# A gated pair's GELU, two block stores and the wo loads of a fused mixer kernel: four edits in the queues of ScalarE, SyncE and GpSimd

## The chip, the cores and the metric

One core of a Trainium2 chip runs the kernel. The metric is the device time of one execution in microseconds. The engines are named as in the profile: PE is TensorE (matmul; PEld is its weight load), DVE is VectorE, ACT is ScalarE, POOL is GpSimd, SP is SyncE, which here only issues transfers. Each engine executes its own queue strictly in order, as the timelines show: an instruction that waits holds up all behind it on that engine.

## What is computed

Two mixers work on the same normalised input, and their sum is added to the input. Cut to what matters:

```python
xn = layernorm(x)                                   # x: 2048 x 512
# A: linear attention, 32 heads of 16
q, k, v = split(xn @ wqkv)
phi(q) = [softmax(q w_phi), softmax(-q w_phi)]      # per head; the same for k
o = phi(q) (phi(k)^T v) / (phi(q) sum(phi(k)))
# B: gated MLP with a spatial matrix
z  = gelu(xn @ w_in)                                # 2048 x 1376
z1, z2 = z[:, :688], layernorm(z[:, 688:])
g  = w_sp @ z2 + b_sp                               # 2048 x 2048 times 2048 x 688
out = x + o @ wo + (z1 * g) @ w_out
```

All is float32. A product is made of three matmuls: each operand is split into a rounded part (`h`, made by ScalarE with a copy to float32r, `round_h`) and the rest (`l`, made by VectorE with a subtraction, `rest_l`), and `mm3` (L51) adds h·h, h·l and l·h.

## The kernel before, in words

The 2048 tokens are 16 tiles of 128. Up to about 300 us the kernel makes the projections of both mixers: `z2` stays on chip (split, as `B`), `z1` before its GELU goes to memory (`z1_d`), and the query features with their sums go to memory as `e_d`.

**The spatial stage** (L790 to L820, about 300 to 506 us) computes `w_sp @ z2` for eight pairs of token tiles, `i` = 0 to 7. One pair is done in four steps of `n` (`NQ`), each over four of the 16 source tiles; a step has seven products `g` in the manner of Strassen (`FORM`, L682), two blocks each, so 42 matmuls. The seven sums of a pair stand in seven of eight PSUM banks. For step `n` + 2 the weights are prepared by `prep_a` (L516): sums of blocks on VectorE (`S`, L530 to L534), then four pieces that ScalarE rounds and VectorE subtracts (`b_parts`, L503); the last piece is `A22`. The weights `wf` are loaded three steps ahead by SyncE (`load_a`, L507). The prepared weights have two sets of buffers, used in turns.

After a pair's fourth step `drain` (L706) takes the seven sums out of PSUM: ScalarE copies the first (L711), VectorE does the rest (L712 to L718). That frees the banks for the next pair, whose first product uses the eighth bank. Then `gate` (L721) applies GELU to the pair's `z1` on ScalarE (L724), multiplies on VectorE (L727), splits the last 48 of the 688 columns into a rounded part and a rest (L728 to L732), and transposes in blocks of 32 (L733). Its `store` writes the result to memory (`u_d`) in four transfers of 32 partitions, each made of runs of 32 numbers (L738). `load_z1` (L689) brings the next pair's `z1` by two transfers from GpSimd into the one buffer `z1t`; since the transposed block of the pair before stands in the same buffer, the load waits for that store.

**The transition.** During the last steps the weights of `w_out` are staged (`stage_w`, L779), and the blocks of the first tiles are loaded (`first_gate`, L766; `first_q`, L774). The store of pair 6 is put off to step `NC` − 2 and issued by SyncE after the loads of `et` (L819). After the spatial stage SyncE loads `u` of tiles 2 and 3 (`fetch_u`, L921), then `wo` in four transfers of 256 KB with a rearranged source (L929); ScalarE and VectorE split each quarter (L930, L931).

**The output stage** (L945 on) goes over the tiles in pairs: `project_u` multiplies the gated block by `w_out` (17 matmuls into `pout`), `attend_T` transposes the query features on TensorE (`ptq`, L863), `attend` multiplies them by the key-value sums (`po`, 32 small matmuls) and splits the result as `oT`, and `project_o` (L902) adds `oT @ wo` (12 matmuls a tile) and writes the tile out. VectorE finishes the features three tiles ahead (`features`, L837), GpSimd copies them to rounded tiles (`er`, L845), and `u` is loaded four tiles ahead. The last pair, 7, is gated late, after tile 9 (`GATE_LAST`, L966); its block, stored by SyncE, is loaded again as `u` of tiles 14 and 15.

**What sets the order.** The launch builds the program with `schedule_with_timeline_sim=True` (L1000): the place of an instruction in its engine's queue comes from a planner that simulates the program, taking the order of the calls as priority. `tc.issue_after(x)` ties instructions behind `x` in the queue of `x`'s engine. So a moved call can land elsewhere in a queue than its line suggests.

Of the kernel before, what the change touches and what calls it, by code (L numbers as in the profile page):

```python
# [10 lines left out]
F32 = mybir.dt.float32  # L11
F32R = mybir.dt.float32r
# [6 lines left out]
P = 128  # L19
S, D, H, DH, FH = 2048, 512, 32, 16, 688  # L20
# [4 lines left out]
NF = 2 * D  # L25
KF = FH // P
REM = FH - KF * P
FU = FH + REM
BL = 32
# [3 lines left out]
NP = NT // 2  # L33
HP, QP = P // 2, P // 4
# [3 lines left out]
def mixer(ctx: ExitStack, tc: tile.TileContext, x, x_t, wv, wqkT, phi_bd, wo, w_in, wst, b_r, w_out, out):  # L38
    nc = tc.nc
    pe, act, dve, pool, sp = nc.tensor, nc.scalar, nc.vector, nc.gpsimd, nc.sync  # L40


    def round_h(eng, h, src):
        if eng is act:
            return act.activation(h, src, AF.Copy).ins  # L45
        return eng.tensor_copy(h, src).ins

    def rest_l(l, src, h, eng=None):
        return (eng or dve).tensor_tensor(l, src, h.bitcast(F32), op=ALU.subtract).ins  # L49
# [19 lines left out]
    e_d = dram.tile([NT, P, NF + 2 * H], F32, name="e_d")  # L69
# [96 lines left out]
    with ExitStack() as p0:  # L166
# [71 lines left out]
        xt, v, rounded, ready = {}, {}, [], []  # L238
# [131 lines left out]
        t = xz.tile([P, 2, FH], F32R, tag="xz", name="xT")  # L370
        xT.append(t)
        x0, pts = xt.pop(0), []
        for k in range(2):
            pts.append(ps.tile([P, 2, P], F32, tag="mm", name="pt"))
            for c in range(2):
                i = pe.transpose(pts[k][:, c], x0[:, (2 * k + c) * P:(2 * k + c + 1) * P], ident).ins
            keep(pe=i)
        warm_up(2)
        for cs, pt in zip(halves, pts):
            src = pt.rearrange("p a b -> p (a b)")  # L380
            i = round_h(act, t[:, 0, cs], src)
# [7 lines left out]
        p = ps.tile([P, D], F32, tag="mm", name="proj")  # L389
# [7 lines left out]
        p = ps.tile([P, D], F32, tag="mm", name="proj")  # L397
# [18 lines left out]
        p = ps.tile([P, D], F32, tag="mm", name="proj")  # L416
# [60 lines left out]
    QW = NF + 7 * H  # L477

    def load_q(s, et):
        load_q.last = sp.dma_start(et[:, :NF + 2 * H], e_d[s]).ins  # L480
        return et

    def q_fin(et, tmp, zb):
# [13 lines left out]
    NQ = NT // QC  # L497
# [3 lines left out]
    SEQ = [(i, q) for i in range(NP) for q in (range(NQ) if i < NP - 1 else (1, 2, 3, 0))]  # L501

    def b_parts(h, l, src):  # L503
        round_h(act, h, src)
        rest_l(l, src, h)

    def load_a(n):  # L507
        i, q = SEQ[n]
        f = []
        for k in range(2):  # L510
            t = ws.tile([P, QC, P], F32, tag=f"f{k}", bufs=2, name="wf")
            sp.dma_start(t, wst[2 * i + k, :, q * QC:(q + 1) * QC, :])
            f.append(t.rearrange("p (k two) t -> p two k t", two=2))
        return f

    def prep_a(n, f):  # L516

        a, b = f
        pl = hl[n % 2]
        ops = {}  # L520

        def parts(names, src):
            t = pl.tile([P, 2, len(names), 2, P], F32R, tag="".join(names), name="A")
            b_parts(t[:, 0], t[:, 1], src)
            for k, m in enumerate(names):
                ops[m] = t[:, 0, k], t[:, 1, k]

        sums = ws.tile([P, 4, 2, P], F32, tag="S", name="S")
        parts(("A11", "A12"), a)
        dve.tensor_tensor(sums[:, 0], b[:, 0], b[:, 1], op=ALU.add)  # L530
        dve.tensor_tensor(sums[:, 1], sums[:, 0], a[:, 0], op=ALU.subtract)  # L531
        parts(("S1", "S2"), sums[:, 0:2])
        dve.tensor_tensor(sums[:, 2], a[:, 0], b[:, 0], op=ALU.subtract)
        dve.tensor_tensor(sums[:, 3], a[:, 1], sums[:, 1], op=ALU.subtract)  # L534
        parts(("S3", "S4"), sums[:, 2:4])
        parts(("A22",), b[:, 1:2])
        return ops
# [3 lines left out]
    with ExitStack() as p1:  # L541
# [45 lines left out]
        for s in range(NE):  # L587
            et = load_q(s, tb.tile([P, QW], F32, tag="et", bufs=2, name="et"))
# [58 lines left out]
    for s in range(NT):  # L647
        p = zproj((kv_ps_p, zc, zbp, za)[s % 4], s, w2, (0, 1) if s % 2 == 0 else (1, 0))
        n = s // 2
        if s % 2 == 0:  # L650
            z2[n] = zw.tile([P, 4, FC], F32, tag="z2", bufs=2, name="z2")
        z = z2[n][:, 2 * (s % 2):2 * (s % 2) + 2]
# [8 lines left out]
        r = zw.tile([P, 1], F32, tag="rstd", bufs=2, name="rstd")  # L661
# [23 lines left out]
    gt = mid.enter_context(right("gt", 1))  # L685
# [20 lines left out]
    def drain(i, g, cb):  # L706
        g = {k: t[:, :FC] for k, t in g.items()}
        b1, b2 = (bias[:, 2 * i + k:2 * i + k + 1] for k in range(2))
        c11, c12, c21, c22 = (cb[:, k, j] for k in range(2) for j in range(2))
        add = lambda o, p, b, q: dve.scalar_tensor_tensor(o, p, b, q, op0=ALU.add, op1=ALU.add)  # L710
        first = act.activation(c12, g["P1"], AF.Copy)  # L711
        add(c11, g["P2"], b1, c12)  # L712
        dve.tensor_tensor(c21, g["P6"], c12, op=ALU.add)
        dve.tensor_tensor(c12, g["P5"], c21, op=ALU.add)
        dve.tensor_tensor(c21, g["P7"], c21, op=ALU.add)  # L715
        add(c22, g["P5"], b2, c21)
        add(c12, g["P3"], b1, c12)
        drained = add(c21, g["P4"], b2, c21)  # L718
        return cb, first.ins, drained.ins

    def gate(i, cb, z, u, ut):  # L721
        cb, first, _ = cb
        with tc.issue_after(first):
            act.activation(z[:, :, :FH], z[:, :, :FH], AF.Gelu_apprx_tanh)  # L724
        zs = z[:, :, :FH].rearrange("p k (j f) -> p k j f", j=2)
        us = u[:, :, :FH].rearrange("p k (j f) -> p k j f", j=2)
        dve.tensor_tensor(us, zs, cb, op=ALU.mult)  # L727
        rm = slice(KF * P, FH)  # L728
        rh = gt.tile([P, 2, REM], F32R, tag="rh", name="rh")
        dve.tensor_copy(rh, u[:, :, rm])  # L730
        rest_l(u[:, :, FH:FH + REM], u[:, :, rm], rh)
        dve.tensor_copy(u[:, :, rm], rh.bitcast(F32))  # L732
        dve.transpose(ut.rearrange("p k f -> p (k f)"), u.rearrange("p k f -> p (k f)"))  # L733

        def store():
            src = ut.rearrange("p k f -> p (k f)")
            dst = u_d[2 * i:2 * i + 2].rearrange("k (j a) t -> a (k j) t", a=BL)
            for b in range(0, P, BL):  # L738
                sp.dma_start(dst[:, :, b:b + BL], src[b:b + BL].rearrange("p (m b) -> p m b", b=BL))

        return store

# [3 lines left out]
    def load_w(src, parts, h, l, t):  # L746
        rows = 0
        for r0, r1 in parts:
            sp.dma_start(t[rows:rows + r1 - r0], src[r0:r1, :])
            rows += r1 - r0  # L750
        return round_h(act, h, t[:rows]), rest_l(l, t[:rows], h)
# [37 lines left out]
    g, es, ets = {}, {}, {}  # L789
    for n in range(NC):  # L790
        i = SEQ[n][0]
        if n % NQ == 1 and i < NP - 1:
            z = load_z1(i)
        products(n, g)
        if n % NQ == NQ - 1 and i < NP - 1:
            c = gt.tile([P, 2, FU], F32, tag="c", name="c")
            cq = c[:, :, :FH].rearrange("p k (j f) -> p k j f", j=2)
            store = gate(i, drain(i, g, cq), z, c, z)
            if i < NP - 2:
                store()  # L800
            g = {}
        if n + 3 < NC:
            raw[n + 3] = load_a(n + 3)
        if n + 2 < NC:
            A[n + 2] = prep_a(n + 2, raw.pop(n + 2))
        if n == NC - 4:
            stage_w()
        if n == NC - 3:
            zs = slot("zb", F32R)
            zb, ident_r = zs[:, :NF].bitcast(F32), zs[:, NF:NF + P]  # L810
            round_h(act, ident_r, ident)
            sp.dma_start(zb, zb_d)
            uT = [first_gate(0)]
            es[0], es[1] = first_q(0), first_q(1)
        if n == NC - 2:
            t = slot("u1", F32R)
            us = {1: load_u(1, k_tiles(t[:, :KF * P]).bitcast(F32), t[:2 * REM, KF * P:(KF + 1) * P])}
            ets[2], ets[3] = (load_q(s, slot("et")) for s in (2, 3))
            with tc.issue_after(load_q.last):  # L819
                store()  # L820
    cb = drain(NP - 1, g, slot("c").rearrange("p (k j f) -> p k j f", k=2, j=2))
    with tc.issue_after(cb[1]), tc.issue_after(cb[2]):
        es[2], last = q_fin(ets.pop(2), slot("qtmp")[:, :NF], zb)
# [4 lines left out]
    gt = p2.enter_context(right("gl", 1))  # L828
    cw = ctx.enter_context(left("cw", 1))
# [3 lines left out]
    def fetch_u(i):  # L833
        return load_u(i, cw.tile([P, KF, P], F32, tag="u", bufs=4, name="u"),
                      cw.tile([2 * REM, P], F32R, tag="rt", bufs=6, name="rt"))
# [82 lines left out]

    GATE_LAST = 8

    for s in (2, 3):  # L921
        us[s] = fetch_u(s)
    wo_h, wo_l = (cw.tile([P, ND, D], F32R, name=f"wo{k}") for k in "hl")
    p = {0: project_u(0, uT.pop(0))}
    fT = attend_T(0)
    with tc.issue_after(lasts[5]), tc.issue_after(lasts[1]), tc.issue_after(fin[-1]):
        for c in range(ND):
            t = cw.tile([P, D], F32, tag="wof", bufs=4, name="wof")
            sp.dma_start(t, wo.rearrange("(k m a r) d -> k a m r d", k=2, a=2, r=QP)[c // 2, c % 2])  # L929
            round_h(act, wo_h[:, c], t)  # L930
            rest_l(wo_l[:, c], t, wo_h[:, c])  # L931
    p[1] = project_u(1, uT.pop(0))
    oT, ins = attend(fT)
    fin.append(ins)
# [10 lines left out]
    for i in range(0, NT, 2):  # L945
# [15 lines left out]
        if i == 2:  # L961
            with tc.issue_after(lasts[6]):
                z = load_z1(NP - 1)
# [40 lines left out]
```

## Time and profile before

| | us |
|---|---|
| median of 3 runs | 653.47 (652.96 to 654.95) |
| the profiled execution, its own time | 652.16 |
| its span, first to last instruction | 650.4 |
| GpSimd busy | 86.2 |
| ScalarE busy | 269.0 |

The time outside the span is 1.8 us. Busy time is a sum over the engine's instructions; matmuls overlap and their ends are modelled, so a busy TensorE is not TensorE at its peak. In a row of a timeline the first number is the start in us from the span's start, the second the time taken, then come engine, line of the kernel, operation, output and input, the count, and in brackets the idle time before it with what ended that. In a row of waits stand the time waited in total, how often, and the longest. In a row of stretches stand the stretch, its length, the busy time of PE, PEld, DVE, ACT and POOL with counts, the granted share of TensorE's clock, the busy share of the 16 DMA engines, and GB/s. In a row of transfers the last number is the median time from issue to landing.

### The profile page before, as it was taken

What the parts mean: (1) busy time and instruction counts of PE and PEld (TensorE: products, weight loads), DVE (VectorE), ACT (ScalarE), POOL (GpSimd) and SP (SyncE); (2) the same over time, 40 slices, a digit from 0 to 9 for tenths busy, and PEclk for the clock granted to TensorE, in tenths of its full rate; (3) what the DMA queues carried; (4) which work ended last, traced back from release to release, by engine and by line L of the source; (5) the groups of instructions that cost most, each with busy time, mean ns of one, the idle gap of its engine ahead of it and who ended that gap; (6) DMA issues with size and microseconds to landing.
All of it is one profiled execution on the core that took longest, in us unless ns stands there. A gap on an engine that the chain in (4) does not pass through costs nothing.

```text
span 650.4 us, 11408 instructions
## 1 busy us (share of the span) xinstructions
PE 627.9 (97%) x4406; PEld 569.9 (88%) x4406; DVE 518.4 (80%) x916; ACT 269.0 (41%) x431; POOL 86.2 (13%) x168
## 2 busy tenths in 40 slices
PE   8999999999999999999999998998999769999998
PEld 6888888888889999999999898998999657777776
DVE  5999979987977699899969678595968569899822
ACT  5643434433324558785343233343335222323220
POOL 4143212111011034440000000000000000100000
PEclk9999999999999999999999998999899969999999
DMA  8345554444356920014455363735559768986921
GB/s 326 141 98 139 134 159 140 112 133 124 88 156 185 324 91 1 2 34 136 102 140 108 129 147 99 163 83 142 104 169 292 174 203 278 316 275 226 248 97 36
DMA packets 94725, 98.39 MB, mean 151 GB/s; under 512 B 52208, under 2 KB 65264, under 8 KB 94672
## 3 DMA queue, kind: packets, MB, share of 16 engines
q1 hardware_dynamic: 84752, 62.81, 34.8%
q0 software_dynamic: 7616, 29.23, 15.2%
q10 hardware_dynamic: 2304, 5.64, 2.3%
q8 instruction: 34, 0.56, 0.3%
q14 instruction: 19, 0.16, 0.1%
HBM read 56.37 MB, written 26.61 MB: 128 GB/s over the span
## 4 chain that ended last, share of the span: by engine, by line
PE 86%; DMA 7%; DVE 3%; issue 2%; SPq 1%; ACT 1%; POOL 0%; ACTq 0%; POOLq 0%; DVEq 0%
PE g L53 9%; PE g L55 9%; PE g L54 9%; PE proj L55 7%; PE proj L53 7%; PE proj L54 7%; PE zps L55 6%; PE zps L53 6%; PE zps L54 6%; PE pout L53 4%; PE pout L54 4%; PE pout L55 4%; DMA wof<-in_wo 2%; DMA z1t<-z_d 2%; DMA et<-e_d 1%
## 5 line engine op out<-in xcount | busy, mean ns | idle before, releaser
L53 PE MATMUL g<-B,A 128*128 128x344 f32 x448 | 145.0, 324 | 6.6 <-DVE c L715 6.6
L54 PE MATMUL g<-B,A 128*128 128x344 f32 x448 | 144.6, 323 | 0.0
L55 PE MATMUL g<-B,A 128*128 128x344 f32 x448 | 144.2, 323 | 0.0
L53 PEld LDWEIGHTS g<-B,A 128*128 128x128 f32 x448 | 85.3, 190 | 8.0 <-DVE c L715 8.0
L54 PEld LDWEIGHTS g<-B,A 128*128 128x128 f32 x448 | 85.3, 190 | 0.0
L55 PEld LDWEIGHTS g<-B,A 128*128 128x128 f32 x448 | 85.3, 190 | 0.0
L45 ACT ACTIVATE A<-S 128x512 fp32r<-128x512 f32 x64 | 39.4, 627 | 70.7 <-DVE S L531 53.0
L49 DVE TENSOR_TENSOR A<-wf,A 128x512 fp32r<-128x512 f32 x64 | 35.4, 554 | 22.8 <-ACT A L45 22.5
L113 ACT ACTIVATE e<-e,r_x 128x1024 f32<-128x1024 f32 x28 | 32.2, 1150 | 49.9 <-DVE e L112 49.9
L53 PE MATMUL proj<-wqk_h,xT 128*128 128x512 f32 x128 | 50.9, 398 | 0.0
L55 PE MATMUL proj<-wqk_h,xT 128*128 128x512 f32 x128 | 50.6, 395 | 0.0
L54 PE MATMUL proj<-wqk_l,xT 128*128 128x512 f32 x128 | 50.3, 393 | 0.0
L49 DVE TENSOR_TENSOR A<-S,A 128x512 fp32r<-128x512 f32 x64 | 43.9, 687 | 7.2 <-ACT A L45 7.0
L53 PE MATMUL zps<-w_0h,xT 128*128 128x344 f32 x128 | 41.4, 323 | 0.0
L55 PE MATMUL zps<-w_0h,xT 128*128 128x344 f32 x128 | 41.1, 321 | 0.0
L53 PE MATMUL zps<-w_1h,xT 128*128 128x344 f32 x128 | 41.0, 320 | 0.0
L55 PE MATMUL zps<-w_1h,xT 128*128 128x344 f32 x128 | 40.9, 320 | 0.0
L54 PE MATMUL zps<-w_0l,xT 128*128 128x344 f32 x128 | 40.9, 319 | 0.0
L54 PE MATMUL zps<-w_1l,xT 128*128 128x344 f32 x128 | 40.9, 319 | 0.0
L45 ACT ACTIVATE A<-wf 128x512 fp32r<-128x512 f32 x64 | 31.8, 514 | 15.3 <-issue 7.2
L116 DVE TENSOR_REDUCE sm<-e 128x64 f32<-128x1024 f32 x28 | 33.9, 1211 | 4.9 <-ACT e L113 4.8
L53 PE MATMUL pout<-woh,oT 128*128 128x512 f32 x60 | 24.6, 410 | 9.9 <-ACT oT L45 9.9
(208 smaller groups left out, 1400.2 us busy)
## 6 DMA issues: line engine op xcount, KB each, us to landing
wf<-in_wst SPq DMA_DIRECT2D x64, 256.0 KB, 3.8
e_d<-e POOLq DMA_DIRECT2D x16, 544.0 KB, 5.2
et<-e_d SPq DMA_DIRECT2D x16, 544.0 KB, 5.5
zacc<-e POOLq DMA_DIRECT2D x12, 512.0 KB, 4.7
er<-et POOLq DMA_DIRECT2D x12, 512.0 KB, 4.9
z_d<-z1f ACTq DMA_DIRECT2D x16, 344.0 KB, 2.2
z1t<-z_d POOLq DMA_DIRECT2D x16, 344.0 KB, 6.0
u_d<-z1t SPq DMA_DIRECT2D x28, 184.0 KB, 4.5
```

The source lines that it names most:

```text
L45: return act.activation(h, src, AF.Copy).ins
L49: return (eng or dve).tensor_tensor(l, src, h.bitcast(F32), op=ALU.subtract).ins
L53: pe.matmul(dst, ah, bh, start=start, stop=False)
L54: pe.matmul(dst, ah, bl, start=False, stop=False)
L55: return pe.matmul(dst, al, bh, start=False, stop=stop).ins
L113: act.activation(e, e, AF.Exp, scale=scale)
L116: dve.tensor_reduce(sm, heads(e), axis=AX.X, op=ALU.add)
```

## The change

GELU of pairs 0 to 6 is now called after the weights of step `n` + 2 have been prepared, and tied on ScalarE behind the last rounding of that preparation (`prep_a.last`, the rounding of `A22`) in place of the drain's copy. The store follows at once, for every pair; pairs 0 to 5 by SyncE as before, pairs 6 and 7 by GpSimd. The remainders are split within `u`: the rounded part goes to the last 48 columns and the rest stays in place, so one copy and the small tile `rh` go. `wo` is loaded with sixteen transfers of 32 rows (64 KB), four to each quarter, by `load_w`, and the loads of `u` for tiles 2 and 3 come after it in the program.

```diff
     def b_parts(h, l, src):
-        round_h(act, h, src)
+        rounded = round_h(act, h, src)
         rest_l(l, src, h)
+        return rounded
...
-            b_parts(t[:, 0], t[:, 1], src)
+            prep_a.last = b_parts(t[:, 0], t[:, 1], src)
...
-    def gate(i, cb, z, u, ut):
+    def gate(i, cb, z, u, ut, after=None):
         cb, first, _ = cb
-        with tc.issue_after(first):
+        with tc.issue_after(after or first):
             act.activation(z[:, :, :FH], z[:, :, :FH], AF.Gelu_apprx_tanh)
...
-        rm = slice(KF * P, FH)
-        rh = gt.tile([P, 2, REM], F32R, tag="rh", name="rh")
-        dve.tensor_copy(rh, u[:, :, rm])
-        rest_l(u[:, :, FH:FH + REM], u[:, :, rm], rh)
-        dve.tensor_copy(u[:, :, rm], rh.bitcast(F32))
+        lo, hi = u[:, :, KF * P:FH], u[:, :, FH:FU].bitcast(F32R)
+        dve.tensor_copy(hi, lo)
+        rest_l(lo, lo, hi)
...
-                sp.dma_start(dst[:, :, b:b + BL], ...)
+                (sp if i < NP - 2 else pool).dma_start(dst[:, :, b:b + BL], ...)
...
-            store = gate(i, drain(i, g, cq), z, c, z)
-            if i < NP - 2:
-                store()
+            cb = drain(i, g, cq)
             g = {}
         if n + 3 < NC:
             raw[n + 3] = load_a(n + 3)
         if n + 2 < NC:
             A[n + 2] = prep_a(n + 2, raw.pop(n + 2))
+        if n % NQ == NQ - 1 and i < NP - 1:
+            gate(i, cb, z, c, z, prep_a.last)()
...
-            with tc.issue_after(load_q.last):
-                store()
...
-    for s in (2, 3):
-        us[s] = fetch_u(s)
...
         for c in range(ND):
-            t = cw.tile([P, D], F32, tag="wof", bufs=4, name="wof")
-            sp.dma_start(t, wo.rearrange("(k m a r) d -> k a m r d", k=2, a=2, r=QP)[c // 2, c % 2])
-            round_h(act, wo_h[:, c], t)
-            rest_l(wo_l[:, c], t, wo_h[:, c])
+            rows = [(m * QP, (m + 1) * QP) for m in range(c // 2 * 8 + c % 2, (c // 2 + 1) * 8, 2)]
+            load_w(wo, rows, wo_h[:, c], wo_l[:, c], cw.tile([P, D], F32, tag="wof", bufs=4, name="wof"))
+    for s in (2, 3):
+        us[s] = fetch_u(s)
```

More of the change, by code (lines that the diff above doesn't have):

```diff
@@ L479, in load_q @@
     def load_q(s, et):
-        load_q.last = sp.dma_start(et[:, :NF + 2 * H], e_d[s]).ins
+        sp.dma_start(et[:, :NF + 2 * H], e_d[s])
         return et
@@ L738, in store @@
             for b in range(0, P, BL):
-                sp.dma_start(dst[:, :, b:b + BL], src[b:b + BL].rearrange("p (m b) -> p m b", b=BL))
+                (sp if i < NP - 2 else pool).dma_start(dst[:, :, b:b + BL], src[b:b + BL].rearrange("p (m b) -> p m b", b=BL))
         return store
```

## The prediction

> **What bounds the kernel now.** I read the page first (span, busy times), then TensorE's waits, then its clock by stretches, then the timelines of each engine around the waits.
>
> ```profile
> span 650.4 us, 11408 instructions
> ...
> PE 627.9 (97%) x4406; PEld 569.9 (88%) x4406; DVE 518.4 (80%) x916; ACT 269.0 (41%) x431; POOL 86.2 (13%) x168
> ```
> ```profile
> PE pout L53 <- ACT oT L45: 9.9, 1, 9.9
> PE g L53 <- DVE c L715: 6.6, 4, 2.7
> ```
> ```profile
> 398.00:401.40 3.40, 3.40 (x14) 3.40 (x13) 3.40 (x7) 0.00 (x0) 0.00 (x0) 0.50 0.23 61
> 456.10:459.40 3.30, 3.30 (x13) 3.30 (x12) 3.30 (x7) 0.00 (x0) 0.00 (x0) 0.50 0.21 55
> 521.00:531.00 10.00, 4.38 (x10) 3.47 (x11) 6.10 (x9) 2.85 (x5) 0.00 (x0) 0.50 0.80 226
> ```
>
> TensorE is busy 97% of the span, so a change can win only where TensorE waits or runs slowly. It waits in two places: four times for the drain of a spatial pair (6.6 us), and once for `oT` before the first output projection (9.9). The third view (column behind the engines: granted clock) adds that after three of these gaps the clock stood at 0.50. Two stretches of 3.4 us at half speed lose 1.7 us each; in the third TensorE works only 4.4 us, losing 2.2. At stake: 6.6 + 3.4 = 10.0 in the spatial stage and 9.9 + 2.2 = 12.1 at the transition, 22.1 in all.
>
> **Part 1, GELU behind the weight roundings.** ScalarE's timeline (start, duration, line), with the idle time and its releaser last:
>
> ```profile
> 304.68 0.46 ACT L711 ACTIVATE c<-g 128x344 f32<-128x344 f32 x1 [0.48 <-PE g L55]
> ...
> 307.89 1.36 ACT L724 ACTIVATE z1t<-z1t 128x1376 f32<-128x1376 f32 x1
> 310.37 0.42 ACT L45 ACTIVATE A<-wf 128x256 fp32r<-128x256 f32 x1 [1.12 <-PE g L55]
> ...
> 357.58 0.46 ACT L711 ACTIVATE c<-g 128x344 f32<-128x344 f32 x1 [0.47 <-PE g L55]
> 364.24 1.35 ACT L724 ACTIVATE z1t<-z1t 128x1376 f32<-128x1376 f32 x1 [6.20 <-DMA z1t<-z_d]
> ...
> 443.17 0.46 ACT L711 ACTIVATE c<-g 128x344 f32<-128x344 f32 x1 [0.48 <-PE g L55]
> 451.16 1.36 ACT L724 ACTIVATE z1t<-z1t 128x1376 f32<-128x1376 f32 x1 [7.53 <-DMA z1t<-z_d]
> ```
> ```profile
> 368.35 0.43 PE L53 MATMUL g<-B,A 128*128 128x344 f32 x1 [1.35 <-DVE c L715]
> ...
> 396.87 0.43 PE L53 MATMUL g<-B,A 128*128 128x344 f32 x1 [1.81 <-DVE c L715]
> ...
> 455.26 0.43 PE L53 MATMUL g<-B,A 128*128 128x344 f32 x1 [2.68 <-DVE c L715]
> ```
> ```profile
> 314.77 1.58 DVE L727 TENSOR_TENSOR c<-z1t,c 128x1376 f32<-128x1376 f32 x1
> ...
> 318.92 1.71 DVE L733 STREAM_TRANSPOSE z1t<-c 128x1472 f32<-128x1472 f32 x1
> ...
> 366.15 0.69 DVE L49 TENSOR_TENSOR A<-wf,A 128x512 fp32r<-128x512 f32 x1 [4.12 <-ACT A L45]
> ...
> 367.78 0.51 DVE L715 TENSOR_TENSOR c<-g,c 128x344 f32<-128x344 f32 x1
> ```
>
> Call t the start of a pair's first drain copy (L711). In the first pair GELU starts at t + 3.2 and TensorE has no gap; in the two others shown it starts at t + 6.66 and 7.99, with gaps of 1.35 and 2.68: each is GELU's offset less 5.3. The chain: GELU waits for its `z1` load, the rounding of the next weights stands behind it on ScalarE, the subtraction of that rounding (366.15) stands ahead of L715 on VectorE, and L715 frees the bank that TensorE wants. The change puts GELU behind all four roundings of that step, so the chain loses its first link. The last rounding cannot run before TensorE has read the old weights (310.37, t + 5.7), so GELU now starts at t + 6.1 at the earliest. What is queued behind it are roundings for the step after, which TensorE wants only two steps (about 13 us) later, and on VectorE the product L727.
>
> Is the `z1` load late next? One load buffer makes a loop: GELU, L727, transpose, store, load, GELU. In the first pair L727 stood at t + 10.1 and the transpose ended at t + 15.9, with GELU at t + 3.2 and VectorE not blocked; GELU at t + 6.1 to 7.5 still precedes that place.
>
> ```profile
> 328.48 1.06 POOL L692 DMA_DIRECT2D z1t<-z_d  x2 [24.72 <-DVE S L534]
> ```
> ```profile
> z1t<-z_d POOLq DMA_DIRECT2D x16, 344.0 KB, 6.0
> u_d<-z1t SPq DMA_DIRECT2D x28, 184.0 KB, 4.5
> u<-u_d SPq DMA_DIRECT2D x15, 320.0 KB, 4.6
> ```
>
> From there the next load went out at 328.48 and lands 6.0 later, 334.5. An undelayed pair takes (357.58 − 304.68)/2 = 26.45, so the next t is 331.1 and the load lands at t + 3.4, before the t + 6.1 at which GELU may start. I take the whole 10.0 away. Dropping the copy of the remainders (0.2 us of VectorE, eight times) I cost at nothing: VectorE has 20% to spare; were that cover gone, 1.6 us.
>
> **Part 2, `wo` in sixteen loads, ahead of two `u` loads; the store of pair 6 off SyncE.**
>
> ```profile
> 482.40 0.86 SPq L749 DMA_DIRECT2D wof<-in_w_out  x2
> ...
> 498.93 6.97 SPq L739 DMA_DIRECT2D u_d<-z1t  x4
> ...
> 509.60 2.76 SPq L929 DMA_DIRECT2D wof<-in_wo  x4
> ```
> ```profile
> 513.00:515.00 2.00, 2.00 (x10) 1.63 (x9) 1.86 (x4) 0.78 (x2) 0.00 (x0) 1.00 0.27 98
> ```
> ```profile
> 515.65 0.63 ACT L45 ACTIVATE woh<-wof 128x512 fp32r<-128x512 f32 x1 [1.87 <-DMA wof<-in_wo]
> ...
> 524.83 0.63 ACT L45 ACTIVATE woh<-wof 128x512 fp32r<-128x512 f32 x1 [2.57 <-DMA wof<-in_wo]
> ...
> 525.99 1.06 ACT L45 ACTIVATE oT<-po 128x512 fp32r<-128x512 f32 x2
> ```
> ```profile
> 506.30 0.40 PE L53 MATMUL pout<-wu,u_uh 128*128 128x512 f32 x1
> ...
> 515.65 1.09 PE L885 MATMUL po<-f,kvT 64*32 64x256 f32 x32
> 526.62 0.79 PE L53 MATMUL pout<-woh,oT 128*128 128x512 f32 x1 [9.87 <-ACT oT L45]
> ```
>
> The rounding of `oT` stands on ScalarE behind four roundings of `wo`, which come 3.1 us apart (515.65 to 524.83), at the pace of the loads. While little else moved (513 to 515) the DMA share was 0.27, that is 4.3 of 16 engines, 98 GB/s: the four 256 KB loads, whose outermost dimension is 4, share four engines. A load of 32 contiguous rows is free of that shape. Sixteen issues replace four, by bounds: 0.43 us each (0.86 / 2, the first two of w_out) to 0.69 (2.76 / 4): 6.9 to 11.0 us. They start when SyncE is free, which without the store is 498.9, or when the buffers under `wof` are, at the latest with the last spatial product (506.2; the row at 506.30 is the first projection).
>
> I take the late start and the quick issue (nothing else is in that queue then): 506.2 + 6.9 = 513.1, last landing with the 4.6 of the `u` loads 517.7, one rounding and one subtraction 0.6 + 0.7, 519.0; but that quarter of `wo` is used only after nine matmuls (2 us). `po` ends at 516.7. So TensorE resumes at about 518.6, a gap of 1.9 in place of 9.9: 8.0 won. Of the half clock I keep 1.7 (a gap of 1.81 was followed by it, one of 1.35 was not): 2.2 − 1.7 = 0.5 won. The two `u` loads that now follow `wo` feed products that stood at 536; they land by about 520, hidden by the output projection of the first two tiles. Sum 8.5. [...]
>
> **Part 3, the stores of pairs 6 and 7 by GpSimd.**
>
> ```profile
> 473.17 1.06 POOL L692 DMA_DIRECT2D z1t<-z_d  x2 [27.86 <-ACT A L45]
> 540.22 0.53 POOL L845 DMA_DIRECT2D er<-et  x1 [65.99 <-DMA xr<-in_x]
> ```
> ```profile
> 602.51 1.13 SPq L739 DMA_DIRECT2D u_d<-zt  x2
> ...
> 611.62 0.38 SPq L754 DMA_DIRECT2D u<-u_d  x1
> ```
> ```profile
> 632.21 0.46 PE L53 MATMUL pout<-wu,uh 128*128 128x512 f32 x1
> ```
>
> No row shows GpSimd issuing such a store: four transfers of 32 × 46 = 1472 runs of 128 bytes. Its transfers of 128 rows take 0.53 us. If that is all fixed, four cost 2.1 us; if it is all per run, 0.53 × 11.5 × 4 = 24.4. I take the middle, 13. Pair 6: GpSimd idles 66 us from 474 to 540, which holds either end. Pair 7 is dearer: the store begins at 602.5, is in memory 4.5 after its last issue, and only then can tile 14's `u` be loaded (today at 611.62; 4.6), rounded and subtracted (0.63 and 0.69 for 512 columns, so 0.8 + 0.9 for 640; some 0.4 of hand-over). With X us of issue that is 602.5 + X + 11.2, and TensorE wants it at 632.2: X up to 18.5 is hidden. At 13, nothing is lost. All later work shifts with TensorE, so this margin stays.
>
> [...]
>
> **Sum.** 652.16 (the profiled run; span 650.4 plus 1.8 around it) − 10.0 − 8.5 = 633.7. The median shown is 653.47, 1.3 above the profiled run: 635.0. Own range 631 to 638.
>
> **The rivals.**
> - *`wo` is bound by issue.* At 0.69 each the loads leave by 517.2 and land by 521.8; with 1.3 of rounding less 2 for the place of use TensorE resumes at 521 to 523, still with its 2.2 of half clock. Some 5 won instead of 8.5: 638.5. [...]
> - *The store of pair 7 is late, yet the change still wins.* X = 24.4: TensorE waits 5.9 and then loses 1.7 to the clock: 642.6. For it: the all-per-run end.
> - *The boundaries stay as they are* (the change does not do what it says): another wait, such as the `wf` load ahead of the drain on VectorE, takes GELU's place at the four gaps. 635.0 + 10.0 = 645.0. Against it: VectorE's wait at 366.15 names the rounding.
> - *Slower, by the GpSimd store.* The 18.5 are used up once X exceeds 18.5 + 18.5 = 37 us, 9.2 us per transfer; at 15 us per transfer TensorE waits 41 us, net about 23 slower (677). Against it: this lies beyond the row's all-per-run end of 24.4.
>
> **How the numbers follow.** Chances: forecast 0.58 (635.0); issue-bound `wo` 0.10; late store, still faster 0.15; boundaries unchanged 0.06; gains and new waits cancel 0.03; slower by the store 0.08. The range runs from 630.5 (nearly all 22.1 won: 653.5 − 22.1 = 631.4) to 643.5 (the late store), and leaves out 0.17. A difference within 0.3% is about what a measurement of this kernel cannot tell from none. Faster: 0.58 + 0.10 + 0.15 + 0.06 = 0.89.
>
> **What would show it.** Step 1: no wait of `g` products for L715, clock 1.00 from 300 to 500, GELU about 6 us behind L711. Step 2: `wo` roundings under 2 us apart, the wait for `oT` near 2 us. Step 3: GpSimd's store instructions, four together under 18 us, and no TensorE wait near the products of tile 14. Wrong if VectorE's product holds the queue so long that weights come late, if `u` of tile 2 now holds ScalarE ahead of `oT`, or if the store instructions run over 5 us each.

## The result, and the profile after

The changed kernel takes 632.95 us (median; 632.66 to 633.23) against 653.22 (652.86 to 654.95) for the kernel before on the same chip: a ratio of 0.9685, 95% interval 0.9667 to 0.9703, 20.3 us less. The profiled execution took 633.23 us with a span of 631.5, against 652.16 and 650.4. The line numbers shift by up to three (GELU is now L725, the drain copy L712).

First come lines of the page, then TensorE's waits, then stretches with the granted clock in the column behind the five engines:

```profile
span 631.5 us, 11445 instructions
...
PE 621.9 (98%) x4406; PEld 564.9 (89%) x4406; DVE 517.8 (82%) x908; ACT 270.9 (43%) x431; POOL 93.7 (15%) x176
```
```profile
PE pout L53 <- ACT oT L45: 2.1, 1, 2.1
...
PE ptq L867 <- DMA er<-et: 1.4, 1, 1.4
```
```profile
300.00:400.00 100.00, 100.00 (x638) 100.00 (x637) 85.44 (x173) 41.95 (x71) 4.38 (x8) 1.00 0.52 133
400.00:500.00 100.00, 100.00 (x634) 99.20 (x633) 78.51 (x156) 37.88 (x68) 6.84 (x10) 1.00 0.64 172
```

The four waits of `g` for the drain are gone and the spatial stage runs at full clock throughout. The wait for `oT` is 2.1 us in place of 9.9. One wait is new: transposes of query features (`ptq`) wait 1.4 us for `er`. TensorE's timeline gives the places where the time went:

```profile
495.24 0.40 PE L53 MATMUL pout<-wu,u_uh 128*128 128x512 f32 x1
...
507.78 0.50 PE L53 MATMUL pout<-woh,oT 128*128 128x512 f32 x1 [2.08 <-ACT oT L45]
...
513.40 1.06 PE L865 MATMUL ptq<-ident,et 128*128 128x128 f32 x5
```
```profile
595.86 1.48 PE L867 MATMUL ptq<-zb,er 128*128 128x128 f32 x15 [1.39 <-DMA er<-et]
```

| stretch, by the first instruction of each | before | after | difference |
|---|---|---|---|
| start to first projection | 506.30 | 495.24 | −11.06 |
| to the first output projection (`oT`) | 20.32 | 12.54 | −7.78 |
| to the next transposes (534.30 before) | 7.68 | 5.62 | −2.06 |
| from there to the end of the span | 116.1 | 118.1 | +2.0 |

ScalarE's timeline shows GELU where the prediction put it, 6.0 us behind the drain copy (so in the first three pairs; 4.5 to 5.7 us in the others), and the four `wo` roundings back to back:

```profile
304.65 0.46 ACT L712 ACTIVATE c<-g 128x344 f32<-128x344 f32 x1 [0.48 <-PE g L55]
310.70 1.34 ACT L725 ACTIVATE z1t<-z1t 128x1376 f32<-128x1376 f32 x1
```
```profile
501.61 2.21 ACT L45 ACTIVATE woh<-wof 128x512 fp32r<-128x512 f32 x4
504.50 0.74 ACT L45 ACTIVATE uh<-u 128x640 fp32r<-128x640 f32 x1 [0.68 <-DMA u<-u_d]
506.50 0.74 ACT L45 ACTIVATE uh<-u 128x640 fp32r<-128x640 f32 x1 [1.26 <-DMA u<-u_d]
507.14 1.07 ACT L45 ACTIVATE oT<-po 128x512 fp32r<-128x512 f32 x2
```

`wo` is rounded by 503.8, before the `po` products end (about 505.7). What is left of the wait is the rounding of tile 3's `u` (506.50), which stands ahead of `oT` on ScalarE and waits for its load.

### The profile page after: what moved, and what is told of

It reads as the page before. It is cut to its first block, busy times and chain, and to the rows that moved or that the text cites. A ratio compares the mean times of both kernels' runs of the same rounds, so it can differ in the third digit from the quotient of the medians.

```text
span 631.5 us, 11445 instructions
## 1 busy us (share of the span) xinstructions
PE 621.9 (98%) x4406; PEld 564.9 (89%) x4406; DVE 517.8 (82%) x908; ACT 270.9 (43%) x431; POOL 93.7 (15%) x176
## 4 chain that ended last, share of the span: by engine, by line
PE 93%; DMA 2%; DVE 2%; SPq 1%; issue 0%; ACT 0%; POOL 0%; DVEq 0%; ACTq 0%; POOLq 0%
PE g L55 11%; PE g L54 11%; PE g L53 11%; PE proj L55 7%; PE proj L53 7%; PE proj L54 7%; PE zps L55 6%; PE zps L53 6%; PE zps L54 6%; PE pout L53 4%; PE pout L55 4%; PE pout L54 4%; DMA er<-et 2%; PE ptq L867 1%; PE kvps L312 1%; SPq L748 1%
## 5 line engine op out<-in xcount | busy, mean ns | idle before, releaser
L54 PE MATMUL g<-B,A 128*128 128x344 f32 x448 | 143.2, 320 | 0.0
L53 PE MATMUL g<-B,A 128*128 128x344 f32 x448 | 143.1, 319 | 0.0
L55 PE MATMUL g<-B,A 128*128 128x344 f32 x448 | 142.9, 320 | 0.0
L53 PEld LDWEIGHTS g<-B,A 128*128 128x128 f32 x448 | 84.2, 188 | 0.0
L55 PEld LDWEIGHTS g<-B,A 128*128 128x128 f32 x448 | 84.1, 188 | 0.0
L54 PEld LDWEIGHTS g<-B,A 128*128 128x128 f32 x448 | 84.1, 188 | 0.0
L45 ACT ACTIVATE A<-wf 128x512 fp32r<-128x512 f32 x64 | 33.3, 521 | 31.7 <-PE g L55 14.9
L869 ACT ACTIVATE f<-ptq 128x512 f32<-128x512 f32 x32 | 16.5, 603 | 47.7 <-PE ptq L867 41.2
```

Of the source, the lines that this page charges most:

```text
L53: pe.matmul(dst, ah, bh, start=start, stop=False)
L54: pe.matmul(dst, ah, bl, start=False, stop=False)
L55: return pe.matmul(dst, al, bh, start=False, stop=stop).ins
L869: lasts[5] = act.activation(f, pt.rearrange("p a k b -> p a (k b)"), AF.Copy).ins
```

## The experiments

The kernels below differ only in order, in transfers or in the remainder split. Each ratio is to the kernel before on the same chip, with its 95% interval.

### GELU: which edit emptied the gaps?

**The tie alone undone.**

```diff
-            gate(i, cb, z, c, z, prep_a.last)()
+            gate(i, cb, z, c, z)()
```

> The changed kernel with one thing undone: GELU of pairs 0 to 6 is called at the new place, after the weights of the next step, but tied to the drain's copy again, so that the planner puts it ahead of the four roundings on ScalarE, as before the change. Theory (order on ScalarE): the gaps of TensorE at the pairs' ends come back, each GELU's offset from the drain's first copy less 5.3, with half-clock stretches behind some: about 10 us slower than the changed kernel, 643 (642 to 644). Rival (the earlier multiplication, transpose and store do it, not the order on ScalarE): no gaps, 633, within 1.

Measured: 637.09 (636.74 to 637.96), ratio 0.9763 (0.9738 to 0.9787). Neither expectation came true. The waits for `g` do not come back:

```profile
PE pout L53 <- ACT oT L45: 4.6, 1, 4.6
...
PE g L53 <- DVE c L716: 0.7, 3, 0.3
```

The first projection starts 1.7 us later than with the tie, and most of the rest is at the transition: pair 6's store goes out at 484.26 in place of 480.45, the `wo` loads behind it take 10.2 us to issue in place of 8.0, and the wait for `oT` of 4.6 is followed by half clock (0.83 granted from 510 to 520 us, 1.7 us lost). So the tie does not by itself explain the 10 us of the spatial stage.

**Tie and place of the call undone.**

```diff
-            cb = drain(i, g, cq)
+            gate(i, drain(i, g, cq), z, c, z)()
...
-        if n % NQ == NQ - 1 and i < NP - 1:
-            gate(i, cb, z, c, z, prep_a.last)()
```

> The change, with gate called right behind the drain again and tied to the drain's copy (so neither the later place nor the tie). Theory: what won in the spatial stage is that GELU stands behind the roundings on ScalarE, and with the tie alone gone the later place of the call still gave that order; with both gone GELU waits for its z1 load ahead of the roundings again, the waits of the g products for L715 come back (about 6.6 us in four gaps, with one to three stretches of half clock): 633 + 7 to 12, so 640 to 645. Rival: the tie was all there was to it, so this kernel is like the one without the tie: 637, g waits under 1 us.

Measured: 636.81 (634.67 to 637.84), ratio 0.9767 (0.9745 to 0.9789), no `g` wait in the list. The theory falls; the time and the waits are those of the rival. ScalarE's queue now has the order of the kernel before (drain copy, GELU, then the next roundings), and yet TensorE does not wait for the drain. ScalarE's timelines tell why. The kernel before, where the GELU ahead of the first row started at 364.24 and the one behind it at 421.77:

```profile
392.76 1.35 ACT L724 ACTIVATE z1t<-z1t 128x1376 f32<-128x1376 f32 x1 [6.66 <-DMA z1t<-z_d]
```

This kernel, where the next one starts at 415.11:

```profile
362.08 1.36 ACT L725 ACTIVATE z1t<-z1t 128x1376 f32<-128x1376 f32 x1 [0.73 <-issue]
...
388.16 1.36 ACT L725 ACTIVATE z1t<-z1t 128x1376 f32<-128x1376 f32 x1 [0.26 <-issue]
```

In the kernel before, GELU follows GELU after 28.5 and 29.0 us, each waiting for `z1`; TensorE needs 26.45 a pair. The loop through the one `z1` buffer (GELU, product, transpose, store, load, GELU) was the slower of the two and set the pace. Here the spacings are 26.1 and 27.0, and `z1` lands soon enough for GELU to start 0.6 to 1.2 us behind the drain's copy. (That copy itself stands later than in the kernel before, at 360.92 instead of 357.58: it is queued behind roundings whose sums on VectorE waited 5.49 us for a load of `wf`. TensorE did not wait for it.) Something left in this kernel shortens the loop, and the remainder edit is the only other part that touches it.

**The new theory: the loop, and two edits that each shorten it.** Three kernels test it: the kernel before with the remainder edit alone, the change without both GELU and remainder edits, and the kernel before with the GELU edits alone.

```diff
-        rm = slice(KF * P, FH)
-        rh = gt.tile([P, 2, REM], F32R, tag="rh", name="rh")
-        dve.tensor_copy(rh, u[:, :, rm])
-        rest_l(u[:, :, FH:FH + REM], u[:, :, rm], rh)
-        dve.tensor_copy(u[:, :, rm], rh.bitcast(F32))
+        lo, hi = u[:, :, KF * P:FH], u[:, :, FH:FU].bitcast(F32R)
+        dve.tensor_copy(hi, lo)
+        rest_l(lo, lo, hi)
```

> The kernel before with the remainder edit alone (two VectorE instructions in place of three in each pair, the split in place). Theory: what sets the pace of the spatial stage is the loop through the one z1 buffer (GELU, product, transpose, store, load, GELU), 28.5 to 29 us a pair where TensorE needs 26.45; the copy that goes stood on that loop ahead of the transpose and, with what it waited behind, was worth 1.1 us a pair, as in the kernel with the GELU edits undone (27.25, 26.08, 26.95, 26.45 between its GELUs). Then the g waits go nearly away with this edit alone: 643 to 646. Rival: the prediction's own price, 0.2 us of VectorE time eight times and hidden: 652 to 653, the g waits still at 6 us or more.

Measured: 643.16 (642.34 to 644.17), ratio 0.9853 (0.9831 to 0.9874): 10 us from the edit that was costed at nothing. The waits for `g` fall from 6.6 to

```profile
PE g L53 <- DVE c L715: 0.5, 1, 0.5
```

VectorE's timeline, before and with this edit, over the same pair:

```profile
346.18 0.69 DVE L49 TENSOR_TENSOR A<-S,A 128x512 fp32r<-128x512 f32 x1
346.79 0.20 DVE L732 COPY c<-rh 128x96 f32<-128x96 f32 x1
346.90 0.42 DVE L49 TENSOR_TENSOR A<-wf,A 128x256 fp32r<-128x256 f32 x1
347.24 0.42 DVE L530 TENSOR_TENSOR S<-wf 128x256 f32<-128x256 f32 x1
347.57 0.42 DVE L533 TENSOR_TENSOR S<-wf 128x256 f32<-128x256 f32 x1
347.91 1.71 DVE L733 STREAM_TRANSPOSE z1t<-c 128x1472 f32<-128x1472 f32 x1
```
```profile
346.38 0.69 DVE L49 TENSOR_TENSOR A<-S,A 128x512 fp32r<-128x512 f32 x1
346.99 1.70 DVE L731 STREAM_TRANSPOSE z1t<-c 128x1472 f32<-128x1472 f32 x1
```

The copy takes 0.2 us, but behind it in VectorE's queue stood three operations on the next weights, and only then the transpose. With the copy gone the transpose follows its input at once, ahead of those three: 1.1 us less in the loop each pair. GELU then starts at 335.59, 362.02 and 389.01 in this kernel (26.4 and 27.0 apart). The store and load that close the loop got shorter too (the median landing of the `z1` loads between 300 and 500 us is 4.9 us instead of 5.9); what of that comes from the earlier store was not separated. TensorE's first projection starts at 497.08, where the kernel before has 506.30 and the change 495.24.

> The change with both the GELU edits (place of the call and tie) and the remainder edit undone; wo in sixteen loads and the GpSimd stores stay. Theory (the loop): without either the loop is at 28.5 us a pair again, g waits of 5 to 7 us with one to three stretches of half clock, 643 (640 to 646). Rival: what replaced the tie in the kernel with the GELU edits undone was the stores or the wo edit and not the remainders: 637 as there, g waits under 1 us.

Its edit is the last two together, the second backwards. Measured: 644.61 (644.34 to 645.8), ratio 0.9879 (0.9855 to 0.9904), as the theory has it. The waits are back, a little above the 5 to 7 us expected, and `z1` is late again: GELU waits for it each time and starts at 364.89, 393.64 and 422.63, 28.8 and 29.0 apart. TensorE's waits:

```profile
PE g L53 <- DVE c L716: 7.4, 6, 2.3
```

> The kernel before with the GELU edits alone (call behind the weights of the step, tie behind the last rounding), three-instruction remainders. Theory (the loop): the tie alone takes 4.6 us out of it (GELU to product 2.4 us instead of 7.0), more than the 2.0 to 2.5 it is too long, so all g waits go and the spatial stage ends 10.5 to 11 us earlier, the transition as before: 653 - 10.9 = 642 (641 to 644). Rival: the tie needs the remainder edit too: 645 or more, with g waits of 2 us or more.

Its edit is the GELU part of the change, put into the kernel before. Measured: 642.40 (641.59 to 642.44), ratio 0.9837 (0.9818 to 0.9857), no `g` wait, GELU at 310.79, 337.19, 363.68: 26.4 to 26.5 apart. The tie takes GELU's wait off the path from the drain to the bank and, since the drain and the weights' subtractions now come first, it shortens GELU to product from 7.0 us (364.24 to 371.26) to 2.4 in the changed kernel (363.60 to 366.02). The first projection starts at 495.32. Either edit alone wins most of the spatial stage (9.2 us of the 11.06 by the remainders, 11.0 by the tie), and together they win it once.

### `wo`: the shape of the loads, their place, and the store

**Four loads of 256 KB as before, in the new place.**

```diff
-            rows = [(m * QP, (m + 1) * QP) for m in range(...)]
-            load_w(wo, rows, wo_h[:, c], wo_l[:, c], cw.tile(...))
+            t = cw.tile([P, D], F32, tag="wof", bufs=4, name="wof")
+            sp.dma_start(t, wo.rearrange("(k m a r) d -> k a m r d", k=2, a=2, r=QP)[c // 2, c % 2])
+            round_h(act, wo_h[:, c], t)
+            rest_l(wo_l[:, c], t, wo_h[:, c])
```

> The changed kernel with wo loaded by the four old transfers (outermost dimension 4), at the new place ahead of the u loads. Theory (a transfer runs on as many engines as its outermost dimension allows, four here): the roundings of wo are again about 3.1 us apart, but the loads begin at 493 instead of 509.6, so the last one lands near 507 and TensorE's wait for oT grows from 2.1 to 3 to 5 us: 634.5 to 636. Rival (the late place behind the store was the whole cost): roundings under 2 us apart and 633, within 0.7.

Measured: 637.35 (636.7 to 638.79), ratio 0.9768 (0.974 to 0.9795), more than the theory gave it. The roundings wait for loads again, and the wait for `oT` is 6.3 us; part of it is the two roundings of `u`, which in this order stand between the last rounding of `wo` (ended at 509.0) and that of `oT` (511.38):

```profile
501.66 1.17 ACT L45 ACTIVATE woh<-wof 128x512 fp32r<-128x512 f32 x2
504.95 0.63 ACT L45 ACTIVATE woh<-wof 128x512 fp32r<-128x512 f32 x1 [2.11 <-DMA wof<-in_wo]
508.38 0.63 ACT L45 ACTIVATE woh<-wof 128x512 fp32r<-128x512 f32 x1 [2.80 <-DMA wof<-in_wo]
```

**Eight loads of 128 KB, each with outermost dimension 2.**

```diff
...
+            for k in range(2):
+                sp.dma_start(t[k * HP:(k + 1) * HP], wo.rearrange("(k b m a r) d -> k a b m r d", k=2, b=2, a=2, r=QP)[c // 2, c % 2, k])
...
```

> The changed kernel with wo loaded by eight transfers of 64 rows, each written with an outermost dimension of 2 (two runs of 32 rows). Theory (engines by the outermost dimension): two engines instead of four, so a quarter of wo every 6 us, the last near 519; TensorE waits some 13 us for oT and then loses about 2 to the half clock: 645 (641 to 648), slower than with four transfers although each is half as big. Rival (smaller transfers, sooner issued, are what helps): between the four and the sixteen, 633 to 635.

Measured: 647.15 (647.05 to 647.94), ratio 0.9914 (0.9886 to 0.9943). The theory holds: twice the transfers with half the outermost dimension are slower, not faster.

```profile
512.02 0.63 ACT L45 ACTIVATE woh<-wof 128x512 fp32r<-128x512 f32 x1 [4.97 <-DMA wof<-in_wo]
518.01 0.63 ACT L45 ACTIVATE woh<-wof 128x512 fp32r<-128x512 f32 x1 [5.37 <-DMA wof<-in_wo]
```

With outermost dimension 4 the last two roundings are 3.4 us apart (3.1 in the kernel before), with 2 they are 4.8 to 6.0, with 32 contiguous rows they are back to back. The rates go with that: while little else moved, the loads with 4 brought 98 GB/s in the kernel before (513 to 515 us) and 101 in the new place (496 to 498, a DMA share of 0.26, 4.2 of 16 engines), those with 2 brought 49 to 55 (497.5 to 507), and those of 32 contiguous rows 145 (496 to 499, a share of 0.47). No other outermost dimension was tried.

**The two `u` loads ahead of `wo` again.** `fetch_u(2)` and `fetch_u(3)` move back above the `wo` loads; nothing else changes.

> The change, with the loads of u for tiles 2 and 3 ahead of the sixteen wo loads in SyncE's queue as before. Theory: wo's place in the queue is a term of its own: it begins some 5 us later than at 493 (the u buffers come free only near the end of the spatial stage, 496, and four issues of 0.45 stand ahead), the wait for oT goes from 2.1 to 5 to 7 and is followed by half clock (1.7): 636 to 640. Rival: only the shape of the transfers counts, since the same bytes must land either way: the wait stays near 2, 633.

Measured: 633.03 (631.87 to 633.8), ratio 0.9707 (0.969 to 0.9724). The rival holds. `wo` starts 3.9 us later (496.95), its last rounding ends at 507.3, and the wait for `oT` is 1.6: then `u` of tile 3 no longer stands in the way, and one delay takes the other's place.

**Pair 6's store back on SyncE.**

```diff
-                (sp if i < NP - 2 else pool).dma_start(dst[...], ...)
+                (sp if i < NP - 1 else pool).dma_start(dst[...], ...)
```

> The change with pair 6's store by SyncE (pair 7's stays on GpSimd). Theory: the store takes about 3.9 us of SyncE's queue from 480.5, the first u loads and et go out that much later, still ahead of their use, and wo starts at 493 to 494 since it waits for its buffers anyway: 633 (632.4 to 634). Rival: SyncE's queue was what held the wo loads in the kernel before, and this store gives back the 3.6 us by which the wait for oT is shorter than with four wo loads: 635 to 637, wo starting at 496 or later.

Measured: 636.54 (636.13 to 637.97), ratio 0.9754 (0.9733 to 0.9776): the rival's time, but not its mechanism. `wo` starts when the theory said. SyncE's timeline of the change, then of this kernel:

```profile
480.74 0.40 SPq L753 DMA_DIRECT2D u_uh<-u_d  x1
...
493.05 7.97 SPq L748 DMA_DIRECT2D wof<-in_wo  x16
```
```profile
479.95 3.95 SPq L738 DMA_DIRECT2D u_d<-z1t  x4
...
485.33 1.00 SPq L753 DMA_DIRECT2D u_uh<-u_d  x1
...
493.32 11.89 SPq L748 DMA_DIRECT2D wof<-in_wo  x16
```

and the stretch in which the `wo` loads are issued, again of the change and of this kernel (the last two columns are the share of the DMA engines and GB/s):

```profile
496.00:499.00 3.00, 3.00 (x15) 2.43 (x14) 3.00 (x4) 0.00 (x0) 0.00 (x0) 1.00 0.47 145
```
```profile
496.00:499.00 3.00, 3.00 (x15) 2.43 (x14) 2.32 (x4) 0.69 (x1) 0.00 (x0) 1.00 0.99 284
```

The store holds SyncE's queue, the loads behind it go out 4.6 us later, and the DMA engines are still full (0.99 instead of 0.47) when `wo` is issued; the sixteen issues take 11.9 us and the wait for `oT` is 5.7. So, each undone alone in the change: the shape of the loads is worth 4.2 of the gap (6.26 without it), the store's move 3.6 (5.67 without it), the order of `wo` and `u` nothing. That 4.2 + 3.6 = 7.8 is just what went (9.87 − 2.08) does not show that they add: no kernel undoes these two alone, and with the old transition behind the GELU edits the gap is 10.79, 8.7 more than in the change.

### The two waits that are left

**Pair 7's store back on SyncE** (`pool if i == NP - 2 else sp` in the line above).

> The changed kernel with the last pair's store (pair 7) issued by SyncE again; pair 6 stays on GpSimd. Theory (the copy er of tile 13 stands behind the store's runs in GpSimd's transfer queue, 10.6 us to landing, and TensorE waits 1.4 for it): that wait goes, 631.5 (631 to 632). Rival (the wait comes from the load on the DMA engines, whoever issues the store): the wait stays, 633.

Measured: 632.78 (631.73 to 634.89), ratio 0.9699 (0.9669 to 0.9729), not told apart from the change. In its profile the wait for `er` is gone and the span is 630.0. GpSimd's stores in the change were short to issue, by the rows of the stored tile (shortest, median and longest of the four in ns):

```profile
L738 POOL DMA_DIRECT2D u_d<-z1t x4: 902/908/947, 480.4 to 483.2; - x4
L738 POOL DMA_DIRECT2D u_d<-zt x4: 902/915/934, 581.3 to 584.3; - x4
```

but the copy of `er` right behind it in GpSimd's queue landed late: issue to landing of the `er` copies is 10.6 us at most in the change, 7.4 here. **`oT` ahead of tile 3's `u`**, then the same with pair 7's store on SyncE:

```diff
-            round_h(act, oT[0][:, qs], po[r])
+            attend.rounded = round_h(act, oT[0][:, qs], po[r])
...
-                nxt[i + 3] = gated(us.pop(i + 3))
+                with ExitStack() as behind:
+                    if not i:
+                        behind.enter_context(tc.issue_after(attend.rounded))
+                        behind.enter_context(tc.issue_after(ins))
+                    nxt[i + 3] = gated(us.pop(i + 3))
```

> The change, with the rounding of tile 3's u tied behind oT's rounding and rest in the first output pair. Theory: of the remaining wait for oT of 2.1 us, 1.3 to 1.4 is the rounding of tile 3's u standing ahead on ScalarE, waiting for its load; without it oT follows the end of po (505.7) as it does in the later pairs, wait 0.7 to 1.0, and 631.8 (631.3 to 632.4). Rival: another link (the subtractions of wo on VectorE, or the load of tile 2's u) ends at about the same time: wait over 1.7, 633.

> The same edit, and the last pair's store by SyncE instead of GpSimd. Theory: the wait for er (1.4 us, ptq) is due to GpSimd's store and is apart from the wait for oT, so both gains add: 633 - 1.2 - 1.4 = 630.4 (629.8 to 631.2), and TensorE has no wait over 1.1 us behind the first 300 us. Rival: the store by SyncE wins nothing in the time (its median was 632.8), because its loss elsewhere makes up for er: 631.8, like the one edit alone.

Measured: 634.96 (632.06 to 636.25), ratio 0.9736 (0.9709 to 0.9764), and 632.29 (631.75 to 632.39), ratio 0.97 (0.9685 to 0.9714). The wait for `oT` falls to 0.74 us in both, as the theory says, but the time does not follow. TensorE's timeline of the first, and the stretches around:

```profile
529.71 0.45 PE L867 MATMUL ptq<-zb,er 128*128 128x128 f32 x4
531.54 1.21 PE L867 MATMUL ptq<-zb,er 128*128 128x128 f32 x12 [1.38 <-DMA er<-et]
```
```profile
529.40:532.80 3.40, 2.02 (x20) 1.75 (x19) 3.30 (x8) 0.77 (x2) 0.00 (x0) 1.00 0.68 236
532.80:536.20 3.40, 3.40 (x9) 2.61 (x9) 3.23 (x3) 1.30 (x3) 1.61 (x3) 0.50 0.96 327
```

TensorE arrives earlier at the transposes of the next pair, waits there 1.4 us for a copy of `er`, and a stretch of half clock follows. The second kernel has the same new wait (1.6 us). So neither theory's time came true, and no version here beats the change by more than the measurement tells apart.

## Why the prediction was right

The forecast was 635.0 us; 632.95 came. Its total was right. The reasons hold in part, and part of the agreement is luck: step 2 has its total from parts that missed in opposite directions, and the remainders, costed at nothing, cost the forecast nothing only because the tie wins the same time.

- **Step 1, GELU behind the roundings: 10.0 forecast, 11.06 in the profile, 10.8 alone (653.22 − 642.40).** The mechanism of the gaps stands: GELU 6.0 us behind the drain copy, no wait for `g`, clock 1.00. It was incomplete: it took the order on ScalarE for the cause and used the `z1` loop only to ask what would be late next. The loop, 28.5 us against TensorE's 26.45, was the cause of the lateness.
- **The remainders, costed at nothing (at most 1.6): the step that failed.** The price was that of the copy's own 0.2 us; the edit moves the transpose past three more operations and is worth 10 us without the tie (643.16 against 653.22). Beside the tie it shows little: the kernel before with the GELU edits alone already has no `g` wait. The change without its remainder edit was not tried.
- **Step 2, `wo`: 8.0 of gap forecast, 7.79 came.** Its parts were off. `wo` starts at 493, not behind the last spatial product, lands in 2.0 us rather than 4.6, and takes 0.50 an issue instead of 0.43. Nor does the resumption at 518.6 follow from the terms named: 519.0 less 2 is 517.0, and what the other 1.6 us stand for is not said. The gap of 2.08 where 1.9 was forecast is no longer `wo`'s: it is tile 3's `u` on ScalarE, close to the fault named at the end of the prediction, which spoke of tile 2.
- **The half clock left over, 1.7: it was 0.** The gap of 2.08 is followed by full clock (507.00 to 510.40, below), so 2.2 were won in place of 0.5. This is luck: in the kernel without GELU and remainder edits a gap of 1.97 at the same place was followed by half clock.
- **Step 3, the GpSimd stores: 13 us taken, 3.6 measured,** 0.91 for each transfer, near the all-fixed end. It cost nothing by its issue, as forecast. But GpSimd's stores took 7.3 and 7.5 us from issue to landing (medians), where the prediction had the 4.5 of SyncE's; the margin of 18.5 held that too. The 1.4 us wait for `er` was not foreseen. In the issue, 0.91 us for 1472 runs stands beside 0.53 for the 128 rows of an `er` copy: 11.5 times the runs, 1.7 times the time.
- **The sum.** 18.5 forecast; 11.06 + 7.78 + 2.06 = 20.9 won and 2.0 given back, 18.9 of span. Of the 2.0, the wait for `er` is 1.4; no wait row shows the rest. The two halves of the change measured apart give 10.8 (GELU edits alone) and 8.6 (653.22 − 644.61, stores and `wo` without GELU and remainder edits), 19.4 of the 20.3.

Of the rivals, the `wo` loads are issued in 8.0 us, not 11, and no late store and no slower kernel came: GpSimd's transfers took 0.91 us each, where the late store has 6.1 (24.4 / 4) and the slower kernel 15, which no run shows. The rival in which the boundaries stay has its time in the kernel without GELU and remainder edits (644.61, forecast 645.0), though not by the `wf` load that it named. The prediction gives its range twice, as 631 to 638 and as 630.5 to 643.5; the result lies in both.

## To carry to other kernels

Where one buffer goes round several engines, add up the loop and set it beside the pace of the bound engine first: if the loop is the longer one (here 28.5 us against 26.45), a small operation on it counts once per round with all that its place in the queue lets in ahead of the next link (here a copy of 0.2 us, 1.1 us a round). Two edits that shorten the same loop need not add (here 9.2 and 11.0 us, 11.06 together); undo them singly and together before crediting either. A transfer moved off a queue is worth the earlier departure of all that stood behind it (here 4.6 us earlier), also where the next important transfer starts at the same time (`wo` at 493.05 and 493.32, a wait for `oT` of 2.1 and 5.7).

## What was not expected of the hardware

**Whether half clock followed a short gap went with where the gap fell.** In the kernel before, the clock changes at 398.0, 401.4, 456.0, 459.4, 520.9 and 531.1, whole multiples of 3.41 us apart (133.1 us are 39 of them). Cut into such stretches, the traces read so (TensorE's busy time is the first number behind the length; then the other engines, the clock, the DMA share and GB/s). The kernel before, with its gap of 1.81 in one stretch:

```profile
394.60:398.00 3.40, 1.59 (x10) 1.30 (x10) 3.33 (x7) 1.90 (x5) 0.00 (x0) 1.00 0.28 77
398.00:401.40 3.40, 3.40 (x14) 3.40 (x13) 3.40 (x7) 0.00 (x0) 0.00 (x0) 0.50 0.23 61
```

The change, whose gap of 2.08 is split between two stretches, and the kernel with both GELU edits undone, whose gap of 3.18 is split too:

```profile
503.50:507.00 3.50, 2.19 (x38) 1.10 (x36) 2.11 (x4) 1.55 (x3) 0.00 (x0) 1.00 0.97 290
507.00:510.40 3.40, 2.62 (x11) 2.08 (x12) 3.13 (x4) 1.21 (x3) 0.00 (x0) 1.00 1.12 334
```
```profile
504.70:508.00 3.30, 1.70 (x35) 0.69 (x34) 1.37 (x3) 1.24 (x2) 0.00 (x0) 1.00 0.99 274
508.10:511.40 3.30, 1.82 (x8) 1.38 (x9) 2.57 (x5) 1.71 (x3) 0.00 (x0) 1.00 1.08 322
511.50:514.80 3.30, 3.30 (x17) 2.70 (x16) 3.09 (x7) 0.00 (x0) 0.00 (x0) 1.00 1.08 352
```

The kernel without GELU and remainder edits, whose gap of 1.97 falls into one stretch:

```profile
516.09:519.50 3.41, 1.44 (x28) 0.81 (x12) 2.16 (x3) 2.18 (x4) 0.00 (x0) 1.00 1.01 300
519.50:522.91 3.41, 3.41 (x10) 2.62 (x9) 3.31 (x6) 0.00 (x0) 0.00 (x0) 0.50 1.07 349
```

In these rows stretches with 1.44 and 1.59 us of work are followed by half clock, those with 1.70 and more are not. Other stretches read the same way: 0.74 (the kernel before, from 452.6) and 1.12 (the kernel without GELU and remainder edits, from 423.9) are followed by half clock; 1.82 (`u` ahead of `wo`, from 505.5), 2.12 (the change, from 592.35) and 2.32 (the kernel before, from 367.3) are not. The one exception seen is the stretch of 529.40 above with 2.02, part of it 128-column transposes; whether these count for less was not tried. The stretches do not begin at the same times in each profiled execution: one begins at 398.0 in the kernel before and one at 519.5 in the kernel without GELU and remainder edits, 35.6 times 3.41 us later. So the gap of 1.97 in that kernel was followed by 3.4 us at half clock, a loss of 1.7 us, and the gaps of 2.08 and 3.18 by none. The four executions with `oT` first took 632.06, 634.47, 635.45 and 636.25 us at mean clocks of 0.999, 0.997, 0.997 and 0.996. One such stretch is 0.0027 of the mean clock (half of 3.41 in 631), so the clocks account for one or so, about half of that spread; the rest is open.
